# Weight words in pieces of their own in DRAM, and a load rate of 330 in the planner

## The chip, the cores and the metric

One core of a Trainium2 chip runs the kernel. The metric is the device time of one execution in microseconds. The engines are TensorE (PE, with its weight loads as PEld), VectorE (DVE), ScalarE (ACT), GpSimd (POOL) and SyncE (SP), which issues all DMAs here.

## What is computed

Three layers follow each other, on 4 batches of 576 positions:

```python
# 1: 8 heads of 64; window 32 (heads 0-3), or 32 steps of 4 (heads 4-7)
attn = softmax(where(mask, q @ k.T / 8, -1e9));  x = heads_joined(attn @ v)      # 4 x 576 x 512
# 2: x_prev is x one position back
xk = mu_k * x + (1 - mu_k) * x_prev;  xr = mu_r * x + (1 - mu_r) * x_prev
k = relu(xk @ w_k)                                                              # 512 -> 1024
x = sigmoid(xr @ w_r) * ((k * k) @ w_v)                                          # 1024 -> 512
# 3
u = x + (x.T @ U @ V).T
out = u + relu(u @ w_ch1) @ w_ch2                                               # 512 -> 2048 -> 512
```

The weights `w_*`, `U` and `V` reach the chip as 64-bit words, and the device makes float32 of them.

## The kernel before, in words

**Work.** Layer 1 goes in *units*: a pair of heads of one batch and one part of its positions (0 to 319 or 320 to 575), 32 in all. Units 0 to 3 run one by one (`attend`), all others by twos (`attend2`). A unit is: scores on PE (L544 or L653), mask and row minimum on DVE (L555 or L664, one instruction for each of 4 or 5 windows), exponentials on ACT (L565 or L672), reciprocals of the sums on DVE (L572 and L573, or L678 and L679), the product with them on POOL (L579 or L683), transposes on PE (L589 or L698), their copy to `pts` on ACT (L350), the product with `v` on PE (L602 or L715), and a copy to `x` on ACT.

Layer 2 goes in 8 chunks of 288 positions. `mix` makes `xk` (POOL subtracts, L345; DVE multiplies and adds, L769). Chunk 0 is multiplied in plain float32: `r_row` (L828), then `k_tile` and `v_part` (L812). Chunks 1 to 7 take operands split in a high and a low half and three matmuls for each product (L815 to L817). Layer 3 follows with the same split (L1036 to L1038, L1113 to L1115).

**Weights.** 20 pieces of 128x512 words (`w1raw`, layer 2) and 32 (`w2raw`, layer 3) are loaded by `cv_load` (L366) to one of 4 buffers `w64`. `cv_bits` turns a piece into float32: one ACT instruction (L383) and four on DVE (L384, L385, L387, L390). `cv_weight` keeps a piece of layer 2 in SBUF; `cv_w2` writes one of layer 3 back to DRAM (`w2f`, L417), from where layer 3 reads it later. `split_weight` makes the halves `wh` and `wl` for chunks 1 to 7. The list `jobs` (L1149 to L1157) names the pieces in the order in which they are converted.

In DRAM `w1raw` and `w2raw` are arrays of 128 rows of 1024 words for each pair of pieces: a row is 8192 bytes, and a piece is the first or the second half of every row.

**Order.** The program first collects operations (`op`), each with an engine, an assumed duration, and what it reads and writes. `plan` then orders them: a list scheduler runs forward over all five engines, backward for the latest times, and again, 10 passes, and keeps the order with the earliest end. For a DMA it takes

```python
begin = max(t + 1300, dma)
dma = begin + o.size / RATE
o.done = dma + 700
```

with `RATE = 285.0` bytes a nanosecond. Where the plan has PE idle for more than 900 ns, it puts multiplications of a zero tile there (L1305, *fillers*), as many as fill half of that. The engines then run the instructions in the order in which the plan wrote them, each waiting for its own operands.

Of the kernel before, what the change touches and what calls it, by code (L numbers as in the profile page):

```python
# [16 lines left out]
P = 128  # L17
# [31 lines left out]
HI_MIN = 2.0**-15  # L49
HI_MAX = 1.875 * 2.0**16  # L50
CW = 512
QKW, VW = 640, 640


# [15 lines left out]
FILL, FILL_FROM, FILL_NS = 0.5, 900.0, 0.453  # L70
PLAN_PRINT = None
PASSES = 10
RATE = 285.0


@with_exitstack
def tile_attention_mix_channel(
# [7 lines left out]
    ytmp = [tc.dram_tile([P, NPAIR, S], F32, name=f"ytmp{b}") for b in range(B)]  # L85
    w2f = [tc.dram_tile([P, 2 * CW], F32, name=f"w2f{i}") for i in range(16)]

# [3 lines left out]
    mu_t = cp.tile([P, 8], F32, name="mu_t")  # L91
    zero = cp.tile([P, CW], F32R, name="zero")
    us = cp.tile([P, NT, P], F32R, name="us")
# [34 lines left out]
    def plan():  # L128
# [58 lines left out]
        def forward(rank):  # L187
# [12 lines left out]
            while len(order) < len(ops):  # L200
# [32 lines left out]
                if e == "SP":  # L233
# [3 lines that stand above are left out]
# [41 lines left out]
        for o in order:  # L278
            if o.eng != "PE":
                continue  # L280
            for x in [x for x in o.first if x.home is ps][:1] or [k[0] for k in o.w if o.spare][:1]:
                ends = sorted((max(u.done for u in y.ops) for y in x.line[: x.at]), reverse=True)
                room = o.at - max([idle_from, *ends[x.bufs - 1 : x.bufs]])
                if room > FILL_FROM:
                    wide = CW if x in o.first else CW - HS
                    o.before = (x, wide, int(FILL * room / (FILL_NS * wide)))
# [47 lines left out]
    def dma(nbytes, fn, r, w):  # L334
        op("SP", 415, fn, r, w, size=nbytes)

    def load(nbytes, fn, key):

        dma(nbytes, fn, [], [key])
# [24 lines left out]
    def cv_load(src, n):  # L364
        raw = Lazy([P, CW], I64, "w64", "w64", 4)
        load(P * n * 8, lambda: nc.sync.dma_start(raw()[:, :n], src), (raw,))  # L366
        return raw

    def cv_bits(raw, n, xt_=None):
        xt_ = xt_ or Lazy([P, CW], F32, "w32", "w32", 3)  # L370

        def words():
            v = raw().bitcast(I32).rearrange("p (n w) -> p n w", w=2)
            return v[:, :n, 0], v[:, :n, 1]

        def x():
            return xt_()[:, :n]

        def xi():
            return x().bitcast(I32)  # L380

        kx, kr = [(xt_,)], [(raw,)]
        act(n, lambda: nc.scalar.activation(x(), f32(words()[1]), AF.Abs), kr, kx)  # L383
        dve(n, lambda: nc.vector.tensor_scalar(x(), x(), HI_MIN, HI_MAX, op0=ALU.max, op1=ALU.min), kx, kx)  # L384
        dve(n, lambda: nc.vector.tensor_scalar(  # L385
            xi(), xi(), 3, 0x3FFFFFFF, op0=ALU.logical_shift_left, op1=ALU.bitwise_and), kx, kx)
        dve(n, lambda: nc.vector.scalar_tensor_tensor(  # L387
            out=xi(), in0=words()[1], scalar=-0x40000000, in1=xi(), op0=ALU.bitwise_and, op1=ALU.bitwise_or),
            kx + kr, kx, two=True)
        dve(n, lambda: nc.vector.scalar_tensor_tensor(  # L390
            out=xi(), in0=words()[0], scalar=29, in1=xi(), op0=ALU.logical_shift_right, op1=ALU.bitwise_or),
            kx + kr, kx, two=True)
        return x, kx
# [6 lines left out]
    def piece(dt, name):  # L400
        return Lazy([P, CW], dt, "w", name, NPIECE)

# [3 lines left out]
    def cv_weight(raw, at):  # L406
        whole_w[at] = piece(F32, "wx")
        cv_bits(raw, CW, whole_w[at])
# [6 lines left out]
    def cv_w2(raw, i, j):  # L415
        x, kx = cv_bits(raw, CW)
        dma(P * CW * 4, lambda: nc.sync.dma_start(w2f[i][:, j * CW : (j + 1) * CW], x()), kx, [("w2f", i, j)])  # L417
# [730 lines left out]
    NW = len(places)  # L1148
    jobs = []  # L1149
    for i, j in places:  # L1150
        jobs.append((w1raw[i][:, j * CW : (j + 1) * CW], CW, lambda raw, i=i, j=j: cv_weight(raw, (i, j))))
    jobs += [
        (w2raw[i][:, j * CW : (j + 1) * CW], CW, lambda raw, i=i, j=j: cv_w2(raw, i, j)) for i in range(16) for j in range(2)
    ]
    jobs.append((upk, NT * RANK, cv_u))
    jobs += [(vpk[:, j * HS : (j + 1) * HS], HS, lambda raw, j=j: cv_v(raw, j)) for j in range(2)]
# [244 lines left out]
```

## Time and profile before

| | |
|---|---|
| median of 3 runs | 763.28 us (762.9 to 763.32) |
| profiled execution | 760.95 us |
| its span, first to last instruction | 759.2 us |
| PE busy | 742.4 us, 98% of the span |
| DVE busy | 573.2 us, 75% |
| ACT, POOL busy | 403.4 us, 394.5 us |
| DMA, mean over the span | 142 GB/s, its queue at work for 43.6% of 16 engines' span |

The profile is of one execution. Busy time is a union: an engine with two instructions in flight counts once. PE's instructions overlap each other, and a float32 matmul of the plan stands as two rows in the trace, so 32 rows of L812 are 16 matmuls of the plan. PEclk is the clock that PE was granted, as a share of 2.4 GHz. The time after "idle before" or in brackets is what an engine waited before an instruction, and for whom.

### The profile page before, as it was taken

The page shows a single profiled execution, that of the slowest core. Times are in us where ns is not written, and L with a number is a line of the kernel's source. Part 1 is how long each engine was busy: PE and PEld are TensorE (multiplying, and loading weights), DVE is VectorE, ACT ScalarE, POOL GpSimd, SP SyncE. Part 2 cuts the span into 40 slices and gives each one's busy share as a digit, 9 for nine tenths or more (in the row PEclk, how much of TensorE's full clock was granted, in tenths as well). Part 3 has the DMA queues.
Part 4 walks back from the last instruction along what each step waited for, and adds up shares of the span by engine and source line. Part 5 has one row for each costly group of instructions (what it writes and reads, how often), then busy time and mean ns, then how long its engine had stood idle before and what let it go on. Part 6 is the DMA issues. An engine that isn't in the chain of part 4 may idle for free. (4 is left out here: it accounts for less than half of the span.)

```text
span 759.2 us, 16202 instructions
## 1 busy us (share of the span) xinstructions
PE 742.4 (98%) x5842; PEld 682.0 (90%) x5842; DVE 573.2 (75%) x1303; ACT 403.4 (53%) x1017; POOL 394.5 (52%) x404
## 2 busy tenths in 40 slices
PE   7899999999999999999999999999999999999997
PEld 5678899999999999999998898888988989898986
DVE  5999989998979863467687888766988865565632
ACT  5678985878586666373445454343453434343310
POOL 1324463746454655365675677644777654456500
PEclk9999999999999999999999999999999999999999
DMA  9777608877676810355653253133522212032001
GB/s 285 228 245 230 193 6 273 248 226 240 209 245 186 275 63 29 126 165 182 201 182 99 83 165 129 56 111 104 178 88 84 84 57 84 29 139 70 15 1 55
DMA packets 54208, 107.56 MB, mean 142 GB/s; under 512 B 5873, under 2 KB 15985, under 8 KB 54129
## 3 DMA queue, kind: packets, MB, share of 16 engines
q1 hardware_dynamic: 54128, 106.54, 43.6%
q8 instruction: 46, 0.75, 0.4%
q14 instruction: 34, 0.27, 0.1%
HBM read 83.97 MB, written 22.54 MB: 140 GB/s over the span
## 5 line engine op out<-in xcount | busy, mean ns | idle before, releaser
L345 POOL TENSOR_TENSOR cl<-sums,ch 128x512 fp32r<-128x512 f32 x72 | 97.3, 1351 | 80.5 <-ACT ch L350 52.8
L1115 PE MATMUL psS<-hl,rh 128*128 128x512 f32 (+1 forms) x320 | 119.4, 373 | 0.4 <-DVE hl L1051 0.2
L1113 PE MATMUL psS<-hh,rh 128*128 128x512 f32 (+1 forms) x320 | 119.2, 373 | 0.2 <-ACT hh L1092 0.2
L1114 PE MATMUL psS<-hh,rl 128*128 128x512 f32 (+1 forms) x320 | 119.1, 372 | 0.0
L350 ACT ACTIVATE ch<-sums 128x512 fp32r<-128x512 f32 (+1 forms) x104 | 57.3, 561 | 100.1 <-DVE sums L470 92.0
L815 PE MATMUL psM<-xk,wh 128*128 128x288 f32 x336 | 101.1, 301 | 0.0
L816 PE MATMUL psM<-xk,wl 128*128 128x288 f32 x336 | 99.1, 295 | 0.0
L817 PE MATMUL psM<-xk,wh 128*128 128x288 f32 x336 | 98.8, 294 | 0.0
L345 POOL TENSOR_TENSOR cl<-st,ch 128x256 fp32r<-128x256 f32 x80 | 66.9, 851 | 57.6 <-PE psM L1038 38.2
L470 DVE TENSOR_TENSOR sums<-st 128x256 f32<-128x256 f32 (+1 forms) x144 | 86.6, 650 | 9.9 <-POOL cl L345 5.8
L345 POOL TENSOR_TENSOR xk<-m,xk 128x288 fp32r<-128x288 f32 x56 | 53.3, 961 | 37.9 <-ACT xk L350 33.8
L1115 PEld LDWEIGHTS psS<-hl,rh 128*128 128x128 f32 x320 | 60.3, 188 | 12.3 <-DVE hl L1093 1.1
L1113 PEld LDWEIGHTS psS<-hh,rh 128*128 128x128 f32 x320 | 60.3, 189 | 10.3 <-ACT hh L1092 0.6
L1114 PEld LDWEIGHTS psS<-hh,rl 128*128 128x128 f32 x320 | 60.3, 188 | 9.6
L815 PE MATMUL psM<-k2s,wh 128*128 128x288 f32 x224 | 67.1, 299 | 0.0
L816 PE MATMUL psM<-k2s,wl 128*128 128x288 f32 x224 | 66.0, 295 | 0.0
L817 PE MATMUL psM<-k2s,wh 128*128 128x288 f32 x224 | 65.9, 294 | 0.0
L815 PEld LDWEIGHTS psM<-xk,wh 128*128 128x128 f32 x336 | 63.0, 188 | 1.1 <-DVE y L877 0.2
L817 PEld LDWEIGHTS psM<-xk,wh 128*128 128x128 f32 x336 | 63.2, 188 | 0.0
L816 PEld LDWEIGHTS psM<-xk,wl 128*128 128x128 f32 x336 | 63.1, 188 | 0.1
L1073 DVE TENSOR_TENSOR ok<-ok,psM 128x256 f32<-128x256 f32 (+1 forms) x96 | 46.4, 504 | 20.2 <-PE psM L1038 18.3
L345 POOL TENSOR_TENSOR k2s<-k,k2s 128x288 fp32r<-128x288 f32 x49 | 45.2, 927 | 26.6 <-ACT k2s L350 23.7
(161 smaller groups left out, 2151.9 us busy)
## 6 DMA issues: line engine op xcount, KB each, us to landing
st<-w2f SPq DMA_DIRECT2D x96, 256.0 KB, 3.0
w<-w2raw SPq DMA_DIRECT2D x32, 512.0 KB, 5.3
w<-w1raw SPq DMA_DIRECT2D x20, 512.0 KB, 5.8
w2f<-w SPq DMA_DIRECT2D x32, 256.0 KB, 2.9
raw<-qk SPq DMA_DIRECT2D x16, 320.0 KB, 7.3
ytmp<-y SPq DMA_DIRECT2D x32, 144.0 KB, 2.3
yb<-ytmp SPq DMA_DIRECT2D x4, 1152.0 KB, 7.1
uf<-us SPq DMA_DIRECT2D x32, 144.0 KB, 1.9
```

Source lines behind the costliest of these rows:

```text
L345: op("POOL", t, lambda: nc.gpsimd.tensor_tensor(out=out_(), in0=a(), in1=b(), op=ALU.subtract), r, w, 40, lock=True)
L350: act(n, lambda: nc.scalar.activation(out_(), in_(), AF.Copy), r, w, psum, strided)
L470: dve(k * Q, lambda: nc.vector.tensor_tensor(out=q(sm_, n, k)(), in0=a(), in1=b(), op=op_), [(s1,), (s2,)], [(sm_, key)], two=True)
L815: nc.tensor.matmul(a, lhsT=wh, rhs=xh, start=start, stop=False)
L816: nc.tensor.matmul(a, lhsT=wl, rhs=xh, start=False, stop=False)
L817: nc.tensor.matmul(a, lhsT=wh, rhs=xl, start=False, stop=stop)
L1073: dve(k * Q, lambda: nc.vector.tensor_tensor(out=out_(), in0=a(), in1=b(), op=op_), r, w, two=True, psum=True)
L1113: nc.tensor.matmul(a, lhsT=wh, rhs=xh, start=(j == 0 and e == 0), stop=False)
L1114: nc.tensor.matmul(a, lhsT=wl, rhs=xh, start=False, stop=False)
L1115: nc.tensor.matmul(a, lhsT=wh, rhs=xl, start=False, stop=(j == 7 and e == 1))
```

## The change

The host lays each piece out by itself: 128 rows of 512 + 16 words, 4224 bytes a row, of which the load reads the first 4096. The bytes loaded, the instructions that load them and everything that is computed stay as they are. The planner's `RATE` goes from 285 to 330, and with it the order on all engines.

```diff
+PAD = 16
-RATE = 285.0
+RATE = 330.0
@@
-        jobs.append((w1raw[i][:, j * CW : (j + 1) * CW], CW, lambda raw, i=i, j=j: cv_weight(raw, (i, j))))
+        jobs.append((w1raw[2 * i + j][:, :CW], CW, lambda raw, i=i, j=j: cv_weight(raw, (i, j))))
@@
-        (w2raw[i][:, j * CW : (j + 1) * CW], CW, lambda raw, i=i, j=j: cv_w2(raw, i, j)) for i in range(16) for j in range(2)
+        (w2raw[2 * i + j][:, :CW], CW, lambda raw, i=i, j=j: cv_w2(raw, i, j)) for i in range(16) for j in range(2)
@@
+    def pieces(w):
+
+        out_ = np.zeros((2 * len(w), P, CW + PAD), np.int64)
+        out_[:, :, :CW] = w.reshape(len(w), P, 2, CW).transpose(0, 2, 1, 3).reshape(-1, P, CW)
+        return out_
+
+    w1raw, w2raw = pieces(w1raw), pieces(w2raw)
```

In the changed kernel every line from 52 on has a number higher by one; the text keeps the numbers of before. Three places show what the new order does.

On DVE, the start. L572 and L573 are the reciprocals of a unit, the first L555 below are the masks of unit 1 (one of five pairs of rows is shown), `w_100` and `w_106` the words of the first and the second weight piece. Before:

```order
L573 RECIPROCAL sm<-sm 128x5
L384 TENSOR_SCALAR wx<-wx 128x512
L385 TENSOR_SCALAR wx<-wx 128x512
L555 ISA pr,mn<-psS,cst_t 128x96
...
L387 SCALAR_TENSOR_TENSOR wx<-w_100,wx 128x512
L390 SCALAR_TENSOR_TENSOR wx<-w_100,wx 128x512
L572 TENSOR_SCALAR sm<-sm 128x5
```

The same place now:

```order
L574 RECIPROCAL sm<-sm 128x5
L385 TENSOR_SCALAR wx<-wx 128x512
L556 ISA pr,mn<-psS,cst_t 128x96
...
L385 TENSOR_SCALAR wx<-wx 128x512
L386 TENSOR_SCALAR wx<-wx 128x512 x2
L388 SCALAR_TENSOR_TENSOR wx<-w_100,wx 128x512
L388 SCALAR_TENSOR_TENSOR wx<-w_106,wx 128x512
L391 SCALAR_TENSOR_TENSOR wx<-w_100,wx 128x512
L391 SCALAR_TENSOR_TENSOR wx<-w_106,wx 128x512
L573 TENSOR_SCALAR sm<-sm 128x5
```

Unit 1's masks moved ahead of the first piece's second instruction, and the second piece is converted with the first, ahead of unit 1's reciprocals.

On PE, the end of chunk 0 (`k` in a name is the squared result of the k tiles; `zero` marks fillers; the rows of 96x128 are transposes of units, the 10 ahead of the first L815 or L816 those of units 8 and 9, or 10 and 11). Before:

```order
L812 MATMUL psM<-k_668,wx 128x288 x8
L698 MATMUL psS<-cst_t,pr 96x128 x10
L812 MATMUL psM<-k_668,wx 128x288 x8
L715 MATMUL psS<-pts,raw 64x64 x20
L653 MATMUL psS<-raw 64x96 x20
L812 MATMUL psM<-k_668,wx 128x288 x16
L1305 MATMUL psS<-zero 128x512 x2
L698 MATMUL psS<-cst_t,pr 96x128 x10
L815 MATMUL psM<-xk,wh 128x288
```

Now:

```order
L813 MATMUL psM<-k_645,wx 128x288 x16
L1306 MATMUL psS<-zero 128x512 x6
L699 MATMUL psS<-cst_t,pr 96x128 x10
L1306 MATMUL psS<-zero 128x512 x2
L716 MATMUL psS<-pts,raw 64x64 x20
L654 MATMUL psS<-raw 64x96 x20
L813 MATMUL psM<-k_645,wx 128x288 x16
L816 MATMUL psM<-xk,wh 128x288
```

The transposes of units 8 and 9 moved behind eight more of chunk 0's matmuls and got six fillers ahead of them and two behind; those of units 10 and 11 moved out of this stretch, to behind 132 of the matmuls of chunk 1. In the whole start (ahead of chunk 1) there are 45 fillers now, 58 before.

On ACT, the exponentials of units 8 and 9 (the rows `pr,sm`), the last k tiles (`rt`, `k`) and the sigmoid (`sg`) with its table load. Before:

```order
L672 ACTIVATE pr,sm<-pr,mn 128x96 x10
L383 ACTIVATE wx<-w_762 128x512
L383 ACTIVATE wx<-w_772 128x512
L857 ACTIVATE rt<-psM 128x288
L350 ACTIVATE x_95<-psS 128x4x64
L859 ACTIVATE k_668<-rt 128x288
L857 ACTIVATE rt<-psM 128x288 x2
L859 ACTIVATE k_668<-rt 128x288 x2
L851 ACT_TABLE_LOAD
L851 ACTIVATE sg<-sg 128x1152
```

Now:

```order
L852 ACT_TABLE_LOAD
L852 ACTIVATE sg<-sg 128x1152
L384 ACTIVATE wx<-w_710 128x512
L351 ACTIVATE x_95<-psS 128x4x64 x2
L858 ACTIVATE rt<-psM 128x288
L860 ACTIVATE k_645<-rt 128x288
L858 ACTIVATE rt<-psM 128x288
L860 ACTIVATE k_645<-rt 128x288
L351 ACTIVATE xk<-m 128x288
L673 ACT_TABLE_LOAD
L673 ACTIVATE pr,sm<-pr,mn 128x96 x5
L384 ACTIVATE wx<-w_792 128x512
```

The exponentials moved from ahead of the last k tiles and the sigmoid to behind both, and behind the table load that leads back from it.

## Rows read from the trace of the kernel before

**Rows 1.** Stretches: length, busy us of each engine, PEclk, DMA share, GB/s.

```profile
0.00:9.00 9.00, 7.54 (x37) 5.52 (x37) 1.63 (x12) 3.40 (x12) 0.32 (x5) 1.00 0.77 250
9.00:44.40 35.40, 27.23 (x304) 21.08 (x303) 33.30 (x105) 22.64 (x76) 8.93 (x10) 0.95 0.82 258
44.40:86.00 41.60, 40.46 (x348) 32.12 (x343) 39.80 (x125) 36.12 (x112) 17.11 (x20) 1.00 0.74 232
86.00:760.00 674.00, 667.17 (x5162) 623.24 (x5160) 498.44 (x1062) 341.27 (x821) 368.09 (x370) 1.00 0.40 128
```

**Rows 2.** Timeline of PE: start and duration in us, instruction, wait before it.

```profile
6.46 2.56 PE L1305 MATMUL psS<-zero 128*128 128x512 f32 x10
10.30 1.04 PE L544 MATMUL psS<-raw 64*64 64x96 f32 x20 [1.27 <-DMA raw<-qk]
...
39.62 3.42 PE L828 MATMUL psM<-xk,wx 128*128 128x288 f32 x8 [2.11 <-DVE xk L769]
...
45.27 8.03 PE L812 MATMUL psM<-xk,wx 128*128 128x288 f32 x32
...
85.45 0.75 PE L698 MATMUL psS<-cst_t,pr 128*96 128x128 f32 x5 [1.14 <-POOL pr L683]
85.96 0.38 PE L815 MATMUL psM<-xk,wh 128*128 128x288 f32 x1
```

**Rows 3.** Timeline of DVE, at three places.

```profile
9.83 1.09 DVE L385 TENSOR_SCALAR wx<-wx 128x512 int32<-128x512 int32 x1
...
11.39 0.26 DVE L555 CUSTOM_DVE_ANT_0 pr<-psS,cst_t 128x96 f32<-128x96 f32 x1 [0.47 <-PE psS L544]
...
43.81 0.51 DVE L769 SCALAR_TENSOR_TENSOR xk<-d,mu_t,x 128x288 f32<-128x288 f32 x1
```

**Rows 4.** Four of SP's first DMAs: issue ns, start us; under each, us to landing.

```profile
L521 SPq DMA_DIRECT2D raw<-qk x1: 392/392/392, 0.7 to 0.7; - x1
...
DMA to landing us min/median/max: 3.3/3.3/3.3
...
L1175 SPq DMA_DIRECT2D cst_t<-cst x1: 417/417/417, 1.2 to 1.2; - x1
...
DMA to landing us min/median/max: 3.9/3.9/3.9
...
L366 SPq DMA_DIRECT2D w<-w1raw x1: 424/424/424, 1.7 to 1.7; - x1
...
DMA to landing us min/median/max: 6.7/6.7/6.7
...
L521 SPq DMA_DIRECT2D raw<-qk x1: 439/439/439, 3.1 to 3.1; - x1
...
DMA to landing us min/median/max: 7.2/7.2/7.2
```

**Rows 5.** Groups of DVE from 9 to 44.4 us: busy us, mean ns, idle before.

```profile
L390 DVE SCALAR_TENSOR_TENSOR wx<-w,wx 128x512 int32<-128x512 int32 x10 | 6.7, 681 | 0.0
L385 DVE TENSOR_SCALAR wx<-wx 128x512 int32<-128x512 int32 x10 | 5.9, 602 | 0.1
L384 DVE TENSOR_SCALAR wx<-wx 128x512 f32<-128x512 f32 x10 | 5.9, 602 | 0.1
```

**Rows 6.** Two stretches around the half clock, columns as in rows 1.

```profile
37.00:40.40 3.40, 1.29 (x8) 1.00 (x7) 3.40 (x8) 0.69 (x1) 0.00 (x0) 1.00 0.75 237
40.50:43.80 3.30, 3.30 (x22) 2.12 (x22) 3.30 (x7) 1.86 (x5) 0.00 (x0) 0.50 0.71 262
```

**Rows 7.** ACT: two groups from 0 to 100 us, then two timeline rows.

```profile
L383 ACT ACTIVATE wx<-w 128x512 f32<-128x512 f32 x20 | 13.2, 670 | 4.6 <-DMA w<-w1raw 4.5
...
L857 ACT ACTIVATE rt<-psM 128x288 f32<-128x288 f32 x10 | 3.9, 400 | 1.1 <-PE psM L812 1.1
...
59.81 0.36 ACT L672 ACTIVATE pr<-pr,mn 128x96 f32<-128x96 f32 x1
...
78.32 1.28 ACT L672 ACT_TABLE_LOAD   x1
```

## The prediction

> **What bounds the kernel now.** I read the stretches first [rows 1]. Behind 86 us TensorE (PE) is busy for 667.2 of 674.0 us at full clock, so from there to the end the kernel is PE's stream of matmuls, and DMA at 128 GB/s is far from mattering. The change has no matmul in it, so whatever it brings has to come ahead of 86 us. There the picture is another one: from 9 to 44.4 us PE has 27.2 us of work in 35.4 (some of that is zero filler), and VectorE (DVE) is busy 33.3 of 35.4; from 44.4 to 86 DVE still has 39.8 of 41.6. So the start belongs to DVE, which rebuilds float32 weights out of the 64-bit words, four instructions a piece, and also does its share of the first attention units.
>
> Next, what PE's early waits end with [rows 2]. The row at 39.62 waits 2.11 us for DVE's `xk`, and the first of the 16 matmuls of L812, with which PE's dense part begins, stands at 45.27. One early row, the scores of unit 1 at 10.30, waits 1.27 us for a DMA, `raw<-qk`. That is the only place where loading is late for PE itself, and DVE hangs on it: its L555 for unit 1 starts at 11.39 [rows 3].
>
> Why is that load late? In the queue's first issues [rows 4] the landing is the start plus the last row: `qk` of unit 0 at 0.7 + 3.3 = 4.0, `cst` at 1.2 + 3.9 = 5.1, the first weight piece at 1.7 + 6.7 = 8.4, `qk` of unit 1 at 3.1 + 7.2 = 10.3. The 496 KB of `cst`, whose rows lie back to back, took 5.1 - 4.0 = 1.1 us; the 512 KB of weight words behind them, half of every row of 8192 bytes, took 8.4 - 5.1 = 3.3.
>
> **The change part by part.** The device does the same DMAs, 52 pieces of 128 rows by 4096 bytes; only their addresses and the order that the planner lays out differ.
>
> *The layout.* At the rate of `cst` a piece would take 1.1 x 512 / 496, or about 1.2 us; at the other end it stays at 3.3. `qk` of unit 1 stands behind the first piece, so it can come up to 2.1 us earlier. I take a little over half, 1.2, because `cst` is only one transfer and the queue is just starting. No other load has PE or DVE waiting in a row I use, so the 51 other pieces are costed at nothing: 667.2 of 674.0 us of matmuls cover the later ones, DVE's backlog those of the first 86 us.
>
> The Trainium skill, page "DMA: Bandwidth & Descriptors", section "Latency and other measured facts", reports HBM copies that slowed at row pitches of 512 KiB and more; a pad of 4 KiB cured that, one of 192 bytes did not, and it calls the channel explanation an inference. Its cure by a few KiB speaks against a pad of 128 bytes, its other advice, to lay tiles out contiguously, for this one; no trace here has pitches of that size. What it would make of the time is the second rival below.
>
> *The start on DVE.* With unit 1's scores 1.2 us sooner, its L555 move from 11.39 to about 10.2. One filler less stands ahead of unit 0 and two fewer ahead of unit 1 (10 took 2.56 us, 0.26 each [rows 2]), which lets both start up to that much sooner. Since DVE idles only 35.4 - 33.3 = 2.1 us in this stretch [rows 1], the most there is to win is that plus about 0.4 from a first start before 9 us: 2.5 us. At the other end, the new order puts L555 of unit 1 directly behind L384; before, L385 stood between and filled the wait with 1.09 us [rows 3]. If the load is not sooner, DVE idles that 1.0 us more. I take -1.7 (-2.5 to +1.0), nearer to the gain, as the measured gap between 1.1 and 3.3 us is wide.
>
> *DVE's work before L812.* Up to the eighth L769 (the last operand that the first L812 needs) the order of before has 10 each of L384, L385, L387, L390; now it has 11, 11, 10 and 9. That is one L384 and one L385 more at 0.60 us each and one L390 fewer at 0.68 [rows 5]: +0.5.
>
> *The half clock.* From 40.5 to 43.8 us PE ran at a granted clock of 0.50, after a stretch with 1.29 us of work in 3.40 [rows 6]. DVE's eighth L769 ended at 43.81 + 0.51 = 44.3 [rows 3], L812 began at 45.27: 0.95 us of lag that the half clock left. In the new order PE is just as thin between units 1 and 3, with fewer fillers, so I give about half of that back: -0.4 (-0.95 to 0; more than 0 is a rival).
>
> *From L812 to the first L815.* Before: 85.96 - 45.27 = 40.7 us, with 1.14 us of wait for POOL's `pr` at 85.45 [rows 2]. Now those transposes (units 10 and 11) stand behind 132 of the L815 to L817, so the wait is covered: -1.1. In exchange six fillers stand ahead of the transposes of units 8 and 9, and two behind them: 6 x 0.26 = +1.5. Are they filler in a hole or in the way? ScalarE (ACT) now does the exponentials of units 8 and 9 behind the sigmoid, so they wait for a table load and for the last k tile. Behind that tile ACT has two short activations (0.40 and about the same), one copy of that size, a table load of 1.28, five exponentials at 0.36, a conversion of 0.67 and five more [rows 7]: 1.2 + 1.28 + 1.8 + 0.67 + 1.8 = 6.8 us. PE has 16 L812 in that time, as many as took 8.03 us at 45.27. The exponentials are done before PE arrives; DVE's reciprocals and POOL's product come behind them. So the fillers are mostly in the way, and the copy to `pts` with two fillers beside it adds a wait, of which I count 0.7. Sum: -1.1 + 1.5 + 0.7 = +1.1 (+0.3, where the fillers fall in a hole that would be there anyway, to +2.2).
>
> *Behind 86 us.* All is re-planned, with the same matmuls. Of the 6.8 us that PE is not busy there a re-plan can win or lose some. No row says which way: 0, with 1 us to either side.
>
> **Sum.** -1.7 + 0.5 - 0.4 + 1.1 + 0 = -0.5 us. The profiled execution took 760.95 us (span 759.2); the median of the runs is 763.28, 2.33 above it. 760.95 - 0.5 + 2.33 = 762.8 us.
>
> **Rivals.**
>
> First, *the loads run like `cst` and the order keeps the gain*: -2.5 on DVE, +0.5, no half clock (-0.95), and fillers that fall in a real hole (+0.4): -2.5, or 760.8 us. For it: rows lying back to back went at three times the rate of the first piece. Against it: DVE has to do the same work by L812, and what it wins is at most its idle time.
>
> Second, *the layout doesn't do what it says*: the pieces land no sooner, and an order made for faster loads waits for them. DVE idles behind the first L384 (+1.0), has its 0.5 more to do, and the middle of the start costs its +1.1: +2.6, or 765.9 us, slower. It decides from the point where `qk` of unit 1 lands after about 10 us. For it: one fast row is all there is. Against it: the same queue carries `cst` at three times the rate. By the pad of 192 bytes that cured nothing on the skill's page "DMA: Bandwidth & Descriptors" ("Latency and other measured facts"), this is the case that would come true.
>
> Third, *one more stretch at half clock*: between unit 1's product and the fillers ahead of L828 PE has little to do, and a stretch like 37.0 to 40.4 brings the 1.2 GHz level, this time where PE is what is late. 3.3 us at half speed lose 1.7; with the term of -0.4 gone, -0.5 + 0.4 + 1.7 = +1.6, or 764.9 us.
>
> **How the numbers follow.** A measurement of this kernel tells about 0.2% (1.5 us) from no change, so "same" is 761.75 to 764.8. The forecast, 762.8, lies in it with 0.47; the first rival 0.30, faster; the second 0.12 and the third 0.11, slower, together 0.23. The range for 8 in 10 takes in the middle of the first rival and most of the third: 760.4 to 765.4.
>
> **What would show it.** The first piece landing within 2.5 us of `cst`, and unit 1's L555 by 10.5 us, show the layout right; no change there is the second rival. DVE busy for over 95% between 9 us and L812, and L812 beginning between 43 and 44.5, show that DVE set the start. Six L1305 with hardly a wait behind them, ahead of the transposes of units 8 and 9, show the filler in the way; a wait of 2 us there would show a hole. A clock of 0.50 later than 20 us tells the half clock. I am wrong in kind if PE's part behind 86 us moves by more than 1.5 us, or if PE waits for DMA rows of weights.

## The result, and the profile after

The changed kernel takes 770.11 us (median of 6 runs) against 763.09 us for the kernel before on the same chip. The ratio is 1.0102 with a 95% interval of 1.0071 to 1.0134: 1.0% slower. The prediction said 762.8 us within 760.4 to 765.4, a gain of 0.5 us, so it was wrong in size and in sign. The profiled execution after took 769.46 us, its span 767.2 (before 760.95 and 759.2).

The stretches after, columns as in [rows 1]:

```profile
0.00:9.00 9.00, 7.22 (x48) 5.38 (x50) 1.96 (x14) 3.74 (x12) 0.46 (x6) 1.00 0.82 288
9.00:44.40 35.40, 30.66 (x320) 23.87 (x315) 34.47 (x113) 23.42 (x78) 11.62 (x12) 0.86 0.79 255
44.40:86.00 41.60, 39.07 (x291) 30.77 (x290) 38.58 (x116) 35.19 (x109) 17.24 (x18) 0.92 0.70 226
86.00:760.00 674.00, 668.13 (x5165) 623.85 (x5164) 500.43 (x1062) 343.31 (x822) 367.69 (x370) 1.00 0.39 127
```

The start did get better: DMA moves 288 GB/s in the first 9 us in place of 250, and PE has 30.7 us of work in the second stretch in place of 27.2, part of it longer because the clock was lower (PEclk 0.86 for 0.95). Two things got worse: PEclk is 0.92 in the third stretch, where it was 1.00, and the last row's 668.13 hides that the work ends later. PE's timeline (start, duration, instruction, wait before it; all line numbers after are higher by one) shows the third stretch:

```profile
42.14 8.03 PE L813 MATMUL psM<-xk,wx 128*128 128x288 f32 x32
...
68.45 1.76 PE L1306 MATMUL psS<-zero 128*128 128x512 f32 x6
70.06 0.71 PE L699 MATMUL psS<-cst_t,pr 128*96 128x128 f32 x5
73.30 0.75 PE L699 MATMUL psS<-cst_t,pr 128*96 128x128 f32 x5 [2.53 <-POOL pr L684]
73.80 1.04 PE L1306 MATMUL psS<-zero 128*128 128x512 f32 x2
74.78 2.40 PE L716 MATMUL psS<-pts,raw 96*64 96x64 f32 x40
77.12 1.88 PE L654 MATMUL psS<-raw 64*64 64x96 f32 x40
78.92 8.95 PE L813 MATMUL psM<-k,wx 128*128 128x288 f32 x32
87.50 0.51 PE L816 MATMUL psM<-xk,wh 128*128 128x288 f32 x1
...
763.28 0.39 PE L1116 MATMUL psS<-hl,rh 128*128 128x512 f32 x1
```

The first L813 (L812 of before) stands at 42.14, where it was 45.27 [rows 2]: 3.1 us gained. The first matmul of chunk 1 stands at 87.50, where it was 85.96: the gain is gone and 1.5 us with it. PE's last matmul ends at 763.67, before at 755.16, so 7.0 of the 8.5 us lie behind chunk 1's first matmul. There PE owes 1.6 us more work (the ten transposes of units 10 and 11, and two fillers). The rest, 5.4 us, is loss. I take as loss, from the trace, what the time from one matmul's start to the next has over the usual interval of its kind (0.13 us for an L816), summed from the first L816 to the end: 14.7 us, before 9.3.

### The profile page after: what moved, and what is told of

It reads as the page before. It is cut to its first block, busy times and chain, and to the rows that moved or that the text cites. A ratio compares the mean times of both kernels' runs of the same rounds, so it can differ in the third digit from the quotient of the medians.

```text
span 767.2 us, 16187 instructions
## 1 busy us (share of the span) xinstructions
PE 748.7 (98%) x5831; PEld 686.5 (89%) x5831; DVE 576.9 (75%) x1303; ACT 405.7 (53%) x1019; POOL 397.0 (52%) x404
## 4 chain that ended last, share of the span: by engine, by line
PE 71%; DVE 15%; ACT 5%; DMA 5%; issue 2%; POOL 2%; DVEq 0%; SPq 0%; ACTq 0%; POOLq 0%
PE psS L1116 8%; PE psS L1115 8%; PE psS L1114 8%; PE psM L1037 7%; PE psM L1039 7%; PE psM L1038 7%; PE psM L816 6%; PE psM L818 6%; PE psM L817 6%; DMA w2f<-w 3%; DVE w L391 2%; DVE pr L665 1%; DVE w L388 1%; PE psM L813 1%; DVE w L386 1%
## 5 line engine op out<-in xcount | busy, mean ns | idle before, releaser
L346 POOL TENSOR_TENSOR cl<-sums,ch 128x512 fp32r<-128x512 f32 x72 | 99.8, 1386 | 83.1 <-ACT ch L351 56.4
L816 PE MATMUL psM<-xk,wh 128*128 128x288 f32 x336 | 101.3, 301 | 0.0
L471 DVE TENSOR_TENSOR sums<-st 128x256 f32<-128x256 f32 (+1 forms) x144 | 88.2, 658 | 9.9 <-POOL cl L346 5.3
L346 POOL TENSOR_TENSOR xk<-m,xk 128x288 fp32r<-128x288 f32 x56 | 53.6, 970 | 41.9 <-ACT xk L351 28.9
L816 PE MATMUL psM<-k2s,wh 128*128 128x288 f32 x224 | 67.2, 300 | 0.1
L816 PEld LDWEIGHTS psM<-xk,wh 128*128 128x128 f32 x336 | 63.0, 188 | 0.8
L346 POOL TENSOR_TENSOR k2s<-k,k2s 128x288 fp32r<-128x288 f32 x49 | 42.7, 872 | 38.9 <-ACT k2s L351 36.9
L1074 DVE TENSOR_TENSOR ok<-ok,psM 128x256 f32<-128x256 f32 (+1 forms) x96 | 46.4, 503 | 19.3 <-PE psM L1039 17.3
```

The source lines that it names most:

```text
L346: op("POOL", t, lambda: nc.gpsimd.tensor_tensor(out=out_(), in0=a(), in1=b(), op=ALU.subtract), r, w, 40, lock=True)
L471: dve(k * Q, lambda: nc.vector.tensor_tensor(out=q(sm_, n, k)(), in0=a(), in1=b(), op=op_), [(s1,), (s2,)], [(sm_, key)], two=True)
L816: nc.tensor.matmul(a, lhsT=wh, rhs=xh, start=start, stop=False)
```

## The experiments

A run's edit shifts its line numbers (a run with the changed layout can show L812 or L813 for the same line); the names behind them tell which row it is. Each ratio is to the kernel before on the same chip.

### Layout and order apart

**e1, the layout alone.**

```diff
-RATE = 330.0
+RATE = 285.0
```

> The pieces lie by themselves as in the changed kernel, but the planner keeps 285 GB/s, so every engine has the order of the kernel before. Theory (the new order costs the time, the layout does not): 761.5 to 763.5 us, the first weight piece landing by 6.5 us and unit 1's scores about 1 us earlier, half clock once at most, L812 to L815 at 40 to 41 us. Rival (the layout with rows of 4224 bytes itself costs, for instance through slower transfers later): 767 to 770 us.

761.1 us, ratio 0.9979 (0.9960 to 0.9998). The order is that of before, and the time is 0.2% shorter. The layout costs nothing and gives a little; by the order's own marks hardly anything moved (unit 1's scores at 9.91 in place of 10.30, the first L812 at 45.23). The first piece landed at 8.0 us, not by 6.5: that part of the expectation was wrong, and is taken up below.

**e2, the order alone.** The kernel before with `RATE = 330.0`.

> The order of the changed kernel (planned at 330 GB/s) on the old layout with halves of rows of 8192 bytes. Theory (the order costs the time): 769 to 773 us, as slow as the changed kernel or up to 3 us slower, since the first pieces land later than the order was made for. Rival (the layout costs): 762 to 765 us.

777.35 us, ratio 1.0188 (1.0158 to 1.0218). The order costs the time. It is even 7.2 us slower than the changed kernel by the medians, so under this order the layout is worth much more than under the old one. That this is so because the order was planned for loads that the old layout does not deliver is only argued. PE's longest wait, ahead of a unit's product in the start, is 4.0 us there:

```profile
27.46 1.33 PE L602 MATMUL psS<-pts,raw 96*64 96x64 f32 x20 [4.03 <-ACT pts L350]
```

That wait does not explain the 7.2 us, since the changed kernel has one of 3.84 us at the same place in a second profile (c13, below). The difference lies behind: from chunk 1's first matmul to the end of PE's last one e2 takes 682.9 us, the changed kernel 676.2 and 677.9 in its two profiles, and PE waits 11.4 us there in place of 5.8 and 8.1.

**e3 and e4, the two parts of the order apart.** Two plans are made, one for each rate; up to chunk 1's first matmul every engine follows the first, from there the second (e4 has the rates the other way round). The diff is cut; `f32r` marks the matmuls of chunks 1 to 7 and of layer 3.

```diff
-RATE = 330.0
+RATE = [285.0, 330.0]
...
+        one, two = parts
+        cut = next(i for i, (o, _) in enumerate(one) if o.eng == "PE" and o.mode == "f32r")
+        head = one[:cut]
+        seen = {o.i for o, _ in head}
+        merged = head + [x for x in two if x[0].i not in seen]
```

> New layout; each engine runs the order of the kernel before up to the first matmul of chunk 1 (86 us) and from there the order planned at 330 GB/s. Theory (about half of the 7 us lost lies ahead of that place, with a hole of 2.5 us and a half clock, and half behind it in small waits): 765 to 767.5 us. Rival A (all of it is lost in the start): 761.5 to 763.5. Rival B (all of it behind): 768.5 to 771.

770.79 us, ratio 1.0109 (1.0085 to 1.0134).

> The other way round: new layout, the order planned at 330 GB/s up to the first matmul of chunk 1, from there the order of the kernel before. Theory (half and half): 765.5 to 768 us, with the 2.5 us wait and the half clock near 74 to 81 us still there. Rival A (all lost in the start): 769 to 771. Rival B (all lost behind): 762 to 764.

765.08 us, ratio 1.0025 (1.0008 to 1.0043). With e1 at 761.1 these are four corners. The new order behind chunk 1's first matmul costs 9.7 us behind the old start (e3 less e1) and 5.0 behind the new one (770.1 less 765.1). The new start costs 4.0 us ahead of the old rest and nothing ahead of the new one. So by the medians more than half is lost behind; by the intervals each of these differences holds to 2 or 3 us. For e3 that is rival B, and my half and half fell; e4 lies between half and half (from 765.5) and its rival B (up to 764). The parts do not add up, by 4.7 us. The profile of e4 is of its fastest run (762.05 us). One stretch of the same length, 94 to 268 us, shows the part behind in one row each; in order: e1, the changed kernel, e3, e4 (busy us of PE first):

```profile
94.00:268.00 174.00, 174.00 (x1759) 170.99 (x1758) 160.60 (x435) 124.86 (x346) 98.03 (x107) 1.00 0.65 209
```

```profile
94.00:268.00 174.00, 170.90 (x1778) 166.09 (x1778) 161.11 (x452) 123.88 (x364) 92.14 (x104) 1.00 0.67 214
```

```profile
94.00:268.00 174.00, 167.40 (x1740) 161.44 (x1740) 161.05 (x448) 121.68 (x360) 91.52 (x102) 1.00 0.67 212
```

```profile
94.00:268.00 174.00, 174.00 (x1759) 170.98 (x1758) 159.07 (x434) 123.15 (x343) 96.36 (x106) 1.00 0.65 210
```

Under the old order PE has no hole at all in these 174 us; under the new one it is idle for 3.1 and 6.6 us. The granted clock is 1.00 in all four. PE's waits in the changed kernel behind 86 us (waited for, us in total, times, longest) say for whom:

```profile
PE psS L716 <- ACT pts L351: 2.1, 6, 0.8
PE psS L1115 <- DVE rl L348: 1.0, 1, 1.0
PE psM L928 <- DVE yl L348: 0.6, 1, 0.6
PE psS L699 <- POOL pr L684: 0.6, 2, 0.5
```

They are many small ones: units whose `pts` or `pr` come late, then rows of layer 3. No single place explains them.

### The hole ahead of chunk 1

**e6, without the six fillers.** `late.before = (None, 0, 0)` for the last transposes ahead of chunk 1.

> The changed kernel without the six fillers ahead of the transposes of units 8 and 9. My prediction held these for work in the way, worth 1.5 us. If so: the wait at 73.30 stays at 2.5 us, all behind it starts 1.5 us sooner, and the time falls to 768 to 769. If they lie in a hole (POOL's product is what is late): the wait for it ends at the same time and the first L816 stays at 87 to 88 us, time 769 to 771.5.

771.85 us, ratio 1.0122 (1.0091 to 1.0153). From its first L813 (43.91) the second transposes come after 31.15 us, and after 31.16 in the changed kernel (73.30 less 42.14); its timeline has a longer wait in the fillers' place:

```profile
75.06 0.75 PE L699 MATMUL psS<-cst_t,pr 128*96 128x128 f32 x5 [3.23 <-POOL pr L684]
```

So the fillers lie in a hole and cost nothing (the time is 0.4 us above the range for that case). What is late is the second half's product on POOL. The changed kernel's timelines of ACT, DVE and POOL show why, in this order:

```profile
69.29 0.36 ACT L673 ACTIVATE pr<-pr,mn 128x96 f32<-128x96 f32 x1
```

```profile
68.44 1.10 DVE L386 TENSOR_SCALAR wx<-wx 128x512 int32<-128x512 int32 x1
69.57 0.69 DVE L388 SCALAR_TENSOR_TENSOR wx<-w,wx 128x512 int32<-128x512 int32 x1
70.35 0.43 DVE L385 TENSOR_SCALAR wx<-wx 128x512 f32<-128x512 f32 x1
70.69 0.69 DVE L391 SCALAR_TENSOR_TENSOR wx<-w,wx 128x512 int32<-128x512 int32 x1
71.30 0.17 DVE L679 TENSOR_SCALAR sm<-sm 128x5 f32<-128x5 f32 x1
71.50 0.19 DVE L680 RECIPROCAL sm<-sm 128x5 f32<-128x5 f32 x1
```

```profile
71.30 0.82 POOL L346 TENSOR_TENSOR xk<-m,xk 128x288 fp32r<-128x288 f32 x1 [2.04 <-ACT xk L351]
72.07 1.17 POOL L684 TENSOR_TENSOR pr<-pr,sm 128x480 f32<-128x480 f32 x1
```

The last exponential ends at 69.65. Its reciprocals are done at 71.69, behind four conversions on DVE; POOL takes its product up at 72.07, behind an `xk`, and PE goes on at 73.30: 3.6 us from the last exponential to PE.

**e5, fillers in the hole.** Nine more, between the two halves of the transposes:

```diff
         def tr(e):
+            for _ in range(9 if (ua, e) == (8, 1) else 0):
+                nc.tensor.matmul(pt[1]()[:, :CW], lhsT=zero[:, :P], rhs=zero[:, :CW], start=True, stop=True)
             for w in range(nw):
```

> The changed kernel with nine more fillers between the first and the second five transposes of units 8 and 9, where PE waited 2.53 us for POOL's product at 73.30; all else stays in its place. Theory (the half clock that followed, 74.0 to 80.8 us, came of that hole and cost about 3.4 us at the head of chunk 1): no clock of 0.50 between 70 and 82 us, the first L816 at 84 to 85.5 us in place of 87.5, and 766 to 768.5 us. Rival (the lost clock is covered, since what is late behind it is DVE, ACT and POOL and not PE): the first L816 sooner but 769 to 771 us all the same. Second rival (fillers don't keep the clock): the half clock stays and the first L816 stands at 87 to 88.

771.3 us, ratio 1.0092 (1.0058 to 1.0127): no gain. The clock did stay at 1.00, and from the first L814 (45.41) to the first matmul of chunk 1 (87.31) there are 41.9 us in place of 45.4. But its start was 3.3 us later, since the first piece had landed at 8.2 us, and a stretch of 3.4 us at 0.50 came at 386 us, behind a wait of 1.6 us for `rl`. That one did not come in place of the other: e6 has both, at 75.8 and at 389.9 us.

**c13, the changed kernel once more.**

> The changed kernel once more, beside the three below. 769 to 772 us. The landing of the first weight piece came 1.4 us behind that of the constants in its first profile, 1.5 in one other execution with this layout and 2.6 to 3.2 in the rest; if this is chance from one execution to the next, it will come out at either here, and the first L813 moves with it (42 or 44 to 45.5 us).

771.01 us (766.49 to 774.56), ratio 1.0106 (1.0069 to 1.0142). The same program's timeline and, under it, a stretch of this execution, then one of the first profile:

```profile
73.40 0.71 PE L698 MATMUL psS<-cst_t,pr 128*96 128x128 f32 x5
76.61 0.75 PE L698 MATMUL psS<-cst_t,pr 128*96 128x128 f32 x5 [2.51 <-POOL pr L683]
...
88.06 0.51 PE L815 MATMUL psM<-xk,wh 128*128 128x288 f32 x1
```

```profile
77.10:83.90 6.80, 6.53 (x99) 5.18 (x98) 6.80 (x26) 5.40 (x17) 3.13 (x4) 1.00 0.47 150
```

```profile
73.99:80.82 6.83, 6.83 (x87) 5.39 (x86) 6.83 (x28) 5.59 (x18) 3.15 (x4) 0.50 0.46 137
```

The hole is the same (2.51 us for 2.53), and the half clock behind it is absent: the way from the first L812 (45.49) to chunk 1 takes 42.6 us in place of 45.4. Other profiles with this order say the same: 45.4 and 45.3 us with the half clock (e6, e14), 42.6 without it (e2). The start is later by 3.3 us, with the first piece landing at 8.1 us and not at 6.4 (3.0 us behind the constants; 1.4 to 1.7 in after, e4, e9 and e10), and with DMA at 239 GB/s in the first 9 us, not 288. So two costs of about 3 us each come and go from one execution of the same program to the next. That e5 gained nothing in the median therefore does not show that something behind takes the clock's 3 us up; with the losses that change from run to run, it stays open what the end would gain.

### Is it 330, or any new order?

The new layout, planned at other rates (only `RATE` differs). Even 286 is another order: lined up with that of 285 in the traces, about 423 of DVE's 1303 instructions and 219 of ACT's 1017 stand out of their place, at 330 402 and 364.

> The new layout planned at 286 GB/s in place of 285 or 330. A rate 0.4% higher moves as much of the order as 330 does. Theory (any re-plan is a new draw: the planner's own end is not what the chip does, and the order of before is a tuned draw): 763 to 772 us, some microseconds above the layout alone (761.1), PE waiting for pts, pr and DVE behind 86 us for 2 to 8 us in all. Rival (330 is too optimistic, and what matters is the rate's distance from what the DMAs do): 760 to 762.5 us, like 285.

> The new layout planned at 331 GB/s. Theory (a new draw each time): anywhere from 761 to 773 us, over 2 us away from the changed kernel's 770.1 with a chance of a half. Rival (too optimistic a rate): 769 to 771, like 330.

> New layout, planned at 260 GB/s. Theory A (any re-plan is a draw): 760 to 772 us, with no order between this and the other rates. Theory B (the higher the rate, the more small waits of PE behind 86 us: 1.9 to 2.7 us of them at 285, 3.5 at 286, 5.8 at 330, 7.5 at 331): 760 to 763 us, with 1.5 to 3.5 us of PE waits behind the first matmul of chunk 1.

> New layout, planned at 300 GB/s. Theory A (a draw): 760 to 772 us. Theory B (rising with the rate): 762 to 765 us with 3 to 5 us of PE waits behind the first matmul of chunk 1.

> New layout, planned at 315 GB/s. Theory A (a draw): 760 to 772 us. Theory B (rising with the rate): 764 to 768 us with 4 to 6 us of PE waits behind the first matmul of chunk 1.

> New layout, planned at 400 GB/s. Theory A (a draw): 760 to 772 us, 767 or less with a chance of a half. Theory B (rising with the rate): 771 us or more with over 7 us of PE waits behind the first matmul of chunk 1.

> New layout, planned at 275 GB/s. From 285 up the medians rose with the rate (761.1, 762.7, 764.7, 767.6, 770.1, 772.9 at 285, 286, 300, 315, 330, 400), but 260 gave 770.4, most of it in the start. Theory A (any order but the one that was there is a worse draw): 762 to 770 us, with 12 us or more lost on PE behind the first matmul of chunk 1 (9.3 to 10.4 at 285). Theory B (a lower rate makes a calmer part behind 86 us): 9 to 11 us lost there, whatever the start does.

> New layout, planned at 240 GB/s. Theory A (a worse draw): 12 us or more lost on PE behind the first matmul of chunk 1, 763 to 773 us. Theory B (a lower rate makes a calmer part behind 86 us): 9 to 11 us lost there.

| rate | median us | ratio to before (95%) | first matmul of chunk 1, us | loss of PE behind it, us | PE busy in 94 to 268 us |
|---|---|---|---|---|---|
| 240 (e18) | 772.5 | 1.0113 (1.0067 to 1.0158) | 89.5 | 15.2 | 172.5 |
| 260 (e9) | 770.4 | 1.0098 (1.0073 to 1.0124) | 91.5 | 12.4 | 174.0 |
| 275 (e17) | 764.9 | 1.0030 (1.0008 to 1.0051) | 83.0 | 13.3 | 172.4 |
| 285 (e1) | 761.1 | 0.9979 (0.9960 to 0.9998) | 85.9 | 10.3 | 174.0 |
| 286 (e7) | 762.7 | 1.0001 (0.9982 to 1.0021) | 84.1 | 12.0 | 172.5 |
| 300 (e10) | 764.7 | 1.0034 (1.0018 to 1.0050) | 83.9 | 15.1 | 170.6 |
| 315 (e11) | 767.6 | 1.0061 (1.0040 to 1.0081) | 88.8 | 12.9 | 173.0 |
| 330 (after) | 770.1 | 1.0102 (1.0071 to 1.0134) | 87.5 | 14.7 | 170.9 |
| 331 (e8) | 768.0 | 1.0059 (1.0036 to 1.0082) | 86.6 | 17.3 | 170.6 |
| 400 (e12) | 772.9 | 1.0153 (1.0115 to 1.0191) | 89.6 | 15.9 | 172.0 |

All nine other orders lose 12 to 17 us of PE behind chunk 1's first matmul, the one of before 9.2 to 10.3 (in before, e1 and e4). In three of the nine profiles some of that is a half clock (an estimate from the matmuls' intervals: 1.5 us at 240 and at 260, 2.8 at 331); without it 260 loses about 11, hardly more than 285, and its time goes in the start (91.5). At 275 and 240 the loss holds below 285 as well, so theory B, that a lower rate makes a calmer part behind 86 us, falls. Its times had come out at 300, 315 and 400, not at 260. At 286 the time lies between the two ranges, and 331 is 2.1 us from 330, as the draw allowed. The medians rise to both sides of 285 (331 alone is out of line), though, which a mere draw (theory A) does not ask for. Whether 285 stands at the bottom because it is near what these loads get or because the planner's other numbers go with it, these runs do not tell. No rate brought a time below that of e1.

### Conversions ahead of the units?

Behind the changed kernel's late `pts` I first saw conversions. Its ACT at 125 us:

```profile
124.83 0.67 ACT L384 ACTIVATE w<-w 128x512 f32<-128x512 f32 x1 [1.64 <-DMA w2f<-w]
125.41 1.06 ACT L351 ACTIVATE pts<-psS 96x512 f32<-96x512 f32 x2
```

The copies stand behind a conversion that waits for its buffer. **e14** lets a unit's steps on ACT and DVE pass up to four conversions behind 86 us; **e15** adds e5's fillers; **e16** is the same rule on the order of 285.

The diff shows the rule and leaves out the marks on the operations:

```diff
+        for i in range(split, len(order)):
+            o = order[i]
+            if not getattr(o, "chain", False):
+                continue
+            j, past, k = i, 0, i - 1
+            while k >= split and i - k < AHEAD_OPS and past < AHEAD_CV:
+                x = order[k]
+                if x.i in need.get(o.i, ()) or (x.eng == o.eng and not getattr(x, "conv", False)):
+                    break
+                if x.eng == o.eng:
+                    j, past = k, past + 1
+                k -= 1
+            if j < i:
+                order.insert(j, order.pop(i))
```

> The changed kernel; behind the first matmul of chunk 1, an attention unit's masks, exponentials, reciprocals and copies to pts are moved ahead of up to four instructions of the weight conversion for layer 3 that stand directly before them on ACT or DVE. Theory (in the new order these conversions hold up the units on in-order engines, and that is the small waits behind 86 us): PE's waits for pts and pr there fall from 2.7 us to under 1, and the time is 1.5 to 3.5 us below the changed kernel beside it. Rival (the waits go elsewhere, to the converted rows or to other instructions of DVE): PE's waits in sum stay at 5 to 6 us, time within 1 us.

773.53 us, ratio 1.0146 (1.0107 to 1.0184): 2.5 us above the changed kernel beside it (c13). PE's waits for `pts` and `pr` are 3.7 us, not under 1.

> The one before, with the nine fillers of the earlier experiment between the two halves of the transposes of units 8 and 9. Theory (the half clock costs 3.4 us at the head of chunk 1 and nothing behind takes it up): no clock of 0.50 between 70 and 86 us, 2.5 to 3.5 us below the kernel without the fillers. Rival (what is late there is DVE, ACT and POOL): within 1 us of it.

776.92 us, ratio 1.0178 (1.0137 to 1.0218): no gain over e14. The clock stayed at 1.00 between 70 and 86 us; 3.4 us at 0.50 came at 390 us.

> The layout alone (planned at 285) with the same rule for the units. Theory: only 0.2 to 0.7 us of waits for pts and pr are there to win behind 86 us, so 760 to 761.5 us, within 1 us of the layout alone (761.1) and below the kernel before by 1 to 3 us. Rival: conversions that come later make others wait, 762 to 764.

766.58 us, ratio 1.0055 (1.0034 to 1.0076). The theory fell in all three, and e16's rival (762 to 764) was too low. PE's waits behind chunk 1's first matmul are 8.5 us in e14, 5.8 and 8.1 in the changed kernel's two profiles; e16 lost 5.5 us against e1. In e16 what was passed now stands in somebody else's way. Its DVE, and PE behind it:

```profile
142.65 0.17 DVE L701 TENSOR_SCALAR sm<-sm 128x5 f32<-128x5 f32 x1
142.86 0.19 DVE L702 RECIPROCAL sm<-sm 128x5 f32<-128x5 f32 x1
142.97 1.15 DVE L406 TENSOR_SCALAR w<-w 128x512 int32<-128x512 int32 x1
144.04 1.21 DVE L405 TENSOR_SCALAR w<-w 128x512 f32<-128x512 f32 x1
145.16 0.68 DVE L408 SCALAR_TENSOR_TENSOR w<-w,w 128x512 int32<-128x512 int32 x1
145.77 0.81 DVE L889 SCALAR_TENSOR_TENSOR k<-psM,rt 128x288 f32<-128x288 f32 x2
```

```profile
146.26 0.40 PE L842 MATMUL psM<-k2s,wh 128*128 128x288 f32 x1 [1.61 <-DVE k L889]
```

Both reciprocals went ahead, three conversions followed in a row, and `k` (L889), from which `k2s` is made, came 1.6 us late for PE. Two such waits for `k` make 3.8 us of e16's loss; e1 has none. There one conversion stands between the two pairs of reciprocals, and `k` comes at 145.24. For e14 the place of the loss was not followed up.

## Why the prediction was wrong

- **The layout, unit 1's load 1.2 us sooner.** In the first profile L555 (now L556) of unit 1 starts at 10.05 (about 10.2 was said), and the first piece lands 1.4 us behind `cst` in place of 3.3. Both are luck. Unit 1's scores started at 8.38, 1.9 us sooner and not 1.2, and L556 then followed DVE's own L385 (8.87, 1.26 us), not the load. And only four of the 18 profiles with this layout have such a landing (last section); c13 landed 3.0 us behind. The reading of 3.3 us as the price of the old layout was too simple: the other fourteen land at 7.8 to 8.7 us, the old layout at 8.4 and 8.5 (before, e2). Nor was 10.30 the only place where PE waited for a load: at 14.08 it waited 0.52 us for `raw<-qk`. The first piece after, then c13's:

```profile
L367 SPq DMA_DIRECT2D w<-w1raw x1: 424/424/424, 1.7 to 1.7; - x1
...
DMA to landing us min/median/max: 4.7/4.7/4.7
```

```profile
L366 SPq DMA_DIRECT2D w<-w1raw x1: 424/424/424, 1.7 to 1.7; - x1
...
DMA to landing us min/median/max: 6.5/6.5/6.5
```

- **The start on DVE, -1.7 + 0.5 - 0.4 = -1.6.** The first L812 moved by -3.1 us in the first profile and by +0.2 in c13; the sum lies between. DVE is busy for 97% of the first row below (from 9 us to the first L813, columns as in [rows 1]), as the prediction asked. In c13 it is not: 30.9 of 36.5 us, 85%, with PE waiting 1.04 and 1.77 us for `raw<-qk` and 3.84 for `pts`. So where the first piece lands late, DVE alone does not set the start. The half clock came at 22.8 to 33.0 us (second row), in the place the third rival named, and there it cost next to nothing: e4, with the same order and as early a landing, has 0.50 for 3.4 us only and its first L812 at 41.83, 0.3 us sooner; PE's short waits for `xk` stand there instead.

```profile
9.00:42.14 33.14, 28.40 (x311) 22.05 (x305) 32.21 (x105) 23.10 (x77) 10.40 (x11) 0.85 0.80 258
22.80:33.00 10.20, 9.37 (x92) 7.80 (x93) 9.44 (x32) 5.63 (x20) 3.21 (x4) 0.50 0.76 240
```

- **From L812 to the first L815, +1.1.** +4.7 us with the half clock (45.4 for 40.7), +1.9 without it (c13). The failed step is "the fillers are mostly in the way" with 0.7 of wait: the wait of 2.53 us at 73.30, which the prediction named as the sign, and e6 show them in a hole. I had followed ACT's queue only and put no price on the queues of DVE and POOL, where the 3.6 us from the last exponential to PE were spent. The third rival, a further half clock, was right in kind by luck only: it struck here, behind that hole, and cost 2.8 us (45.4 less 42.6), not the 1.7 I gave it for another place.
- **Behind 86 us, 0 with 1 us to either side.** This is the step that made the prediction wrong: 5.4 us more loss in the profiles, 5.0 to 9.7 us by the corners e1, e3 and e4. The prediction's own sign for this (more than 1.5 us) was passed with 7.0. "No row says which way" was not so. [rows 1] had PE at 667.2 of 674.0 us, and 4.8 of the 6.8 us not busy lie behind PE's last matmul, which ended at 755.16; a re-plan had some 2 us of holes to win. From 94 to 268 us, before, there was hardly any:

```profile
94.00:268.00 174.00, 173.90 (x1756) 170.59 (x1755) 159.23 (x434) 123.63 (x346) 97.84 (x107) 1.00 0.67 208
```

With the same matmuls, an order that leaves the bound engine no hole has hardly anything to gain there and much to lose; the range should have lain mostly on one side.
- **The second rival** (the layout doesn't do what it says, and the order waits) was met by e2, at a price of some 14 us over before in place of 2.6. The Trainium skill, page "DMA: Bandwidth & Descriptors", section "Latency and other measured facts", reports that at a row pitch of 4 MiB a pad of 192 bytes did not restore the rate. No run here has such a pitch. Here rows of 4224 bytes, each piece by itself, did bring the mean time of the first piece's packets from 238 and 228 ns (before, e2) to 160 to 199 in the 18 profiles. Pad and placement were not tried apart.

What is shown: the order and not the layout costs the time, and about half of it or more behind chunk 1's first matmul. What is only argued or stays open: which property of the new order makes the many small waits (the one cause that I tried fell), and how much of the half clock's 3 us reaches the end.

## What to carry to other kernels

Where an order is planned from assumed durations, a change of one number of the planner is a new order of the whole program; cost it as such, and judge it by where the bound engine has holes. Where that engine has none, a new order has little to win and can lose: eight of the nine new orders here clearly did. Measure a change of data layout and a change of the plan apart: here the one gave 0.2%, and the other took 1.2% on the new layout and 1.9% on the old.

## What the runs showed of the hardware

The time of one load in the start differs between executions of the same program. With the new layout the first piece's 128 packets began between 4.1 and 4.4 us in all 18 profiled executions; in four of them the last ended by 6.1 us, in fourteen between 7.0 and 7.9 (before and e2 8.1). In both kinds half of the packets were through by 5.6 us; the late landings are a tail of packets, most of which follow each other by 0.1 to 0.3 us when nine in ten of all are done. With the order of 330 and the new layout the first L812 stood at 41.8 and 42.1 us in the two profiles with an early landing, and at 43.9 to 47.9 in the five with a late one.

The granted clock after the same stretch of work and the same wait of 2.5 us went to 0.50 in two profiles (after, e14) and stayed at 1.00 in three (c13, e2, e4); of the after and c13 profiles the program is the same.
